# Keys of the later batches split and transposed per chunk in one piece instead of two halves, in a block-sparse attention with a cosine MLP

## The chip, the core and the metric

The kernel runs on one core of a Trainium2 chip. The metric is the device time of one execution in microseconds. TensorE is called PE, VectorE DVE, ScalarE ACT, GpSimd POOL, and SyncE SP; SP issues nearly all DMAs, one after the other, from one queue.

## The reference

```python
batch, n_heads, seq, head_dim = (4, 8, 768, 64)       # block = 32, window = 1, three sampled blocks per row of blocks
scores = scale * np.matmul(q, k.transpose(0, 1, 3, 2))
mask = np.abs(blk_i - blk_j) <= window
mask = mask | (blk_i == 0) | (blk_j == 0) | (blk_i == n_blocks - 1) | (blk_j == n_blocks - 1)
mask[qb * block:(qb + 1) * block, kb * block:(kb + 1) * block] = True      # for the sampled kb of each qb
scores = np.where(mask, scores, -1000000000.0)
attn = np.exp(scores - np.max(scores, axis=-1, keepdims=True))
attn = attn / (np.sum(attn, axis=-1, keepdims=True) + 1e-09)
x = np.matmul(attn, v).transpose(0, 2, 1, 3).reshape(B * S, H * D)         # 3072 x 512
h = x @ w_in                                                               # 512 x 2048
return ((h * np.cos(h)) @ w_out).astype(np.float32)                        # 2048 x 512
```

## The kernel before

**Arithmetic.** Every float32 operand of a matmul is scaled and split into a float16 high part and a float16 remainder, and products are summed from these parts. For keys, `k_hi` writes the high part (ACT, by `hi`, L1274) and `k_lo` the remainder (DVE, by `lo`, L1277) into a tile of the class `kn`, of which there are two; `k_transpose` lets a DMA transpose write the tile into `W`, the transposed keys of the current batch. `W` exists once, so the keys of a new batch replace those of the old one.

**Tiling.** The 768 rows of a batch are six chunks of 128: five sparse ones (chunk 0 to 4 of a batch, numbered 6b to 6b+4 over all batches) and a dense one (6b+5) with the first and last blocks. A sparse chunk has four units of two heads each; a dense chunk has eight units of one head. A unit runs through: scores on PE (`sparse_scores`, L1520 to L1526, or `dense_scores`, L1537), bias and maximum on DVE (L1553), exponential on ACT (L1575), split into high part (ACT, L1585) and remainder (DVE, L1589), a DMA transpose of the probabilities (`PT<-ring`, L1604), and the product with the values (L1614 to L1640). Units 0 and 1 of a sparse chunk use heads 0 to 3 (the first half of `W`), units 2 and 3 use heads 4 to 7. Before a sparse chunk, `k_gather` copies the sampled columns of `W` into `Wg`, partly on DVE and partly on ACT (L1366); for the first chunk of batches 1 to 3 it does so in two halves of four heads.

When two chunks are done, their result is transposed by DMA (`xT<-n`, L1669), and a feed-forward step `m` follows for these 256 rows: per step 16 blocks of 12 matmuls (`up`, L1801), cosine on ACT (L1828) between operations of DVE, and 16 blocks of 6 matmuls (`down`, L1851). There are 12 such steps. Exponential and cosine need different tables on ACT, and each change is an `ACT_TABLE_LOAD`.

**Order.** The program is written out in an order that a planner works out beforehand. `plan_kernel` creates steps with an engine, a cost and a due position; `Plan.run` simulates five engines and always takes, of the steps that could start now, the one with the smallest position. `NUDGES`, a table of some 2700 numbers, shifts the position of each kind of step, of each step number, and of single steps. Each engine executes its own steps in that order and waits wherever a step's inputs or its tile are not ready.

**Exchange of keys.** For batch b+1, `load_k` brings the keys into three `stage` tiles, squares them, spreads the maximum over all partitions with a small matmul (L1305) and makes the scale. `prep_k(b + 1, half, pos)` then creates the split and the transposes: with `half` 0 or 1 for six tiles of 128 keys by four heads, two of which share one `kn` tile; with `half` None (until now only for batch 0) for whole tiles of 128 keys by eight heads. In batch 0 the whole form also has switches for single tiles: other tile classes (`KCL`), the remainder on POOL (`KLP`), and the transpose on PE (`KPE`). The functions that the change touches:

Of the kernel before, what the change touches and what calls it, by code (L numbers as in the profile page):

```python
# [57 lines left out]
    idx=3.61, sx=-0.42, regs=-2.95, regs0=-8.34, regs0_0=-6.69, regs1=6.82, regs1_0=-17.04, regs2=3.29, regs2_0=-20.5, regs0_1=-6.69, const=-17.11,  # L58
    kload=-0.63, kload0=-0.87, kload0_0=-10.62, ksq=9.39, ksq0=-7.31, ksq0_0=-21.27, kload0_1=-7.01, ksq0_1=-41.01, kload0_2=-66.32, ksq0_2=11.5,
    kred=-0.92, kall=1.38, kall0=-31.15, ksc=-0.19, ksc0=-12.07, regs3=21.51, regs3_0=25.08, regs4=9.54, regs4_0=-19.9, regs1_1=-20.28, regs2_1=3.97,  # L60
    regs3_1=-8.55, regs4_1=15.17, vload=9.28, vload0=-15.15, vload0_0=11.52, vsq=-6.11, vsq0=13.32, vsq0_0=4.72, vload0_1=2.59, vsq0_1=-3.92,
    vload0_2=38.86, vsq0_2=14.54, vred=42.82, vred0=3.99, vall=1, vall0=-0.62, vsc=-5.56, vsc0=-4.67, ql=-0.06, ql0=11.94, qsq=-0.33, qsq0=17.87,
    qsc=-3.82, qsc0=1.9, qu=0.12, qnu=-14.73, qnu0=-6.95, qhi=2.68, qlo=2.81, qlo0=1.37, uT=-0.62, uT0=-18.36, up=2.32, up0=11.32, khi=4.75,
    khi0=9.03, klo=14.9, klo0=12.03, kT=-0.1, kT0=-22.55, kT0_2=4.55, kp=4.16, kp0=0.97, kp0_2=2.55, kT0_3=-0.33, kp0_3=6.32, kT0_4=22.41,
    kp0_4=39.57, kT0_5=6.88, kp0_5=4.01, vhi=0.82, vhi0=13.51, vhi0_0=0.77, vlo=6.66, vlo0=-1.79, vlo0_0=32.44, vst=10.44, vst0=38.45, vst0_0=-44.56,
    vhi0_1=-13.35, vlo0_1=34.43, vst0_1=-3.14, vlo0_2=0.6, vst0_2=29, vhi0_3=4.95, vlo0_3=9.17, vst0_3=-0.45, vhi0_4=-0.81, vst0_4=-36.52,
    vhi0_5=3.24, vlo0_5=22.52, vst0_5=5.35, vg=2.22, vg0=-25.12, vg0_0=11.42, vg0_1=3.7, vg0_2=-0.77, vi=-2.42, vi0=-1.84, vi0_0=-2.26, vi0_1=-10.33,
    vi0_2=9.28, vi0_3=23.96, wgd=-0.98, wgd0=-12.88, wga=3.36, wga0=1.25, wl=-2.63, wl0=-13.24, wc=-1.9, wc0=-0.7, wc0_0=8.57, wc0_1=-15.78,
    wc0_2=-17.45, wsq=-0.65, wsq0=-1.13, wl1=6.28, wc1=13.61, wc1_0=9.36, wc1_1=-9.88, wc1_2=-12.47, wsq1=13.17, wl2=-47.49, wl3=-7.45, wc3=3.57,
# [453 lines left out]
def plan_kernel(env, B, H, S, D, DM, DFF, pr):  # L523

    pl = Plan()
# [5 lines left out]
    HH = H // 2  # L531
# [28 lines left out]
    def upos(n, j):  # L560
        return unit_pos[n, j]
# [15 lines left out]
    regs = {}  # L577
# [59 lines left out]
    def prep_k(b, half, pos):  # L637
# [1292 lines left out]
```

## Time and profile before

| what | value |
|---|---|
| runs, not profiled | 857.53, 850.83, 858.05 us (median 857.53) |
| profiled execution, own time | 853.78 us |
| its span, first to last instruction | 851.5 us |
| mean granted clock of PE | 0.936 |
| busy: PE, DVE, ACT, POOL | 727.7, 644.8, 624.8, 101.8 us |
| DMA queue q1 (issued by SP) | 308080 packets, 129.35 MB, 73.1% of 16 engines |
| `ACT_TABLE_LOAD` at L1828, L1575 and L1274 | 18, 17 and 1 of 1283 ns each |
| key splits of four heads, ACT and DVE | 36 each |
| transposes of four heads into `W` | 36 |

In the views below a row names the start and the length in us, the engine, the line and the operation with its output and input tiles; a bracket behind it gives the idle time ahead of it on its engine and what ended that. SPq is SP's queue of issues. Batch 0 is exchanged for batch 1 around 243 to 270 us, for batch 2 around 424 to 454, and for batch 3 around 615 to 645.

### The profile page before, as it was taken

Reading aid. Unit: us, or ns where it says so; the run is one execution under the profiler, and the core shown is the slowest. Engines: PE = TensorE matmul, PEld = TensorE weight load, DVE = VectorE, ACT = ScalarE, POOL = GpSimd, SP = SyncE. Lnnn points to the kernel's source line nnn. Section 1 sums busy time; section 2 is a strip of 40 time slices with the busy share of each in tenths; the row PEclk is TensorE's granted clock in tenths of the full one; section 3 lists DMA queues with packets and bytes.
Section 4 is the critical chain, followed back from the end, with each engine's and each line's share of the span. In section 5 each row is a group of like instructions: output and inputs, shape, how many; then the busy total and the mean of one; then the engine's idle time right before and its main releaser. Section 6 shows DMA issues by size and latency. Waiting matters only on the chain.

```text
span 851.5 us, 23033 instructions
## 1 busy us (share of the span) xinstructions
PE 727.7 (85%) x9272; PEld 506.8 (60%) x9272; DVE 644.8 (76%) x1632; ACT 624.8 (73%) x1193; POOL 101.8 (12%) x128
## 2 busy tenths in 40 slices
PE   3556667779999869987999979999988869999997
PEld 2444554546767537656767548677665548576583
DVE  3999989998967776878668876879578746867352
ACT  1686846888867898788758978779669857769342
POOL 5211231000030101200020111000020111000000
PEclk9965697879999979999999999999999989999999
DMA  9999893398895989899979999989696997855300
GB/s 253 324 208 275 211 264 98 73 233 166 213 222 127 201 164 194 157 230 149 228 159 182 196 177 170 216 133 165 191 156 116 184 196 155 181 83 118 87 2 25
DMA packets 313306, 146.54 MB, mean 172 GB/s; under 512 B 266224, under 2 KB 290928, under 8 KB 313200
## 3 DMA queue, kind: packets, MB, share of 16 engines
q1 hardware_dynamic: 308080, 129.35, 73.1%
q0 software_dynamic: 5120, 15.73, 8.4%
q8 instruction: 72, 1.18, 0.6%
q14 instruction: 34, 0.28, 0.1%
HBM read 68.23 MB, written 12.58 MB: 95 GB/s over the span
## 4 chain that ended last, share of the span: by engine, by line
PE 40%; ACT 12%; DMA 11%; DVE 10%; issue 3%; SPq 1%; DVEq 0%; ACTq 0%
PE ph L1801 19%; PE po L1851 15%; DMA PT<-ring 6%; ACT P L1575 4%; DVE P L1553 3%; DMA W<-kn 2%; DMA xT<-n 2%; ACT ring L1585 2%; DVE ring L1589 1%; PE xp L1640 1%; PE xp L1626 1%; PE sp L1520 1%; DVE hs L1833 1%; DVE g L1842 1%; DVE g L1824 1%
## 5 line engine op out<-in xcount | busy, mean ns | idle before, releaser
L1801 PE MATMUL ph<-xT,w 128*128 128x256 f16 x2304 | 270.8, 278 | 10.1 <-DMA xT<-n 6.7
L1851 PE MATMUL po<-w,g 128*128 128x512 f16 x1152 | 269.0, 383 | 8.6 <-ACT g L1839 7.1
L1801 PEld LDWEIGHTS <-w 128*128 128x128 f16 x2304 | 226.5, 99 | 47.6 <-issue 7.3
L1851 PEld LDWEIGHTS <-g 128*128 128x128 f16 x1152 | 108.2, 98 | 128.0 <-ACT g L1839 7.4
L1575 ACT ACTIVATE P<-P,sm 128x352 f32<-128x352 f32 (+1 forms) x224 | 151.9, 679 | 28.8 <-DVE sm L1570 19.3
L1492 POOL DMA_INDIRECT V<-scr,gidx x80 | 89.2, 1115 | 613.4 <-PE xp L1614 316.0
L1589 DVE TENSOR_TENSOR ring<-P,ring 128x704 f16<-128x704 f32 (+1 forms) x112 | 100.1, 906 | 31.5 <-ACT ring L1585 30.1
L1810 ACT ACTIVATE hs<-ph,sm 128x512 f32<-128x512 f32 x96 | 64.4, 680 | 50.8 <-PE ph L1801 42.8
L1585 ACT CAST ring<-P 128x704 f16<-128x704 f32 (+1 forms) x112 | 86.5, 785 | 13.0 <-DMA PT<-ring 11.9
L1553 DVE CUSTOM_DVE_ANT_1 P<-sp,bias 128x352 f32<-128x352 f32 x160 | 77.7, 518 | 14.1 <-PE sp L1526 13.1
L1833 DVE SCALAR_TENSOR_TENSOR hs<-hs,sm,g 128x1024 f32<-128x1024 f32 x48 | 61.0, 1281 | 23.6 <-ACT g L1828 22.4
L1520 PE MATMUL sp<-W,U 128*128 128x192 f16 x320 | 53.2, 268 | 29.2 <-DVE sm L1553 27.7
L1828 ACT ACTIVATE g<-g,sm 128x1024 f32<-128x1024 f32 x48 | 54.7, 1146 | 23.7 <-DVE g L1824 23.4
L1842 DVE TENSOR_TENSOR g<-hs,g 128x1024 f16<-128x1024 f32 x48 | 58.6, 1223 | 17.1 <-ACT g L1839 16.9
L1839 ACT ACTIVATE g<-hs 128x1024 f16<-128x1024 f32 x48 | 50.4, 1051 | 18.2 <-DVE hs L1833 17.5
L1824 DVE SCALAR_TENSOR_TENSOR g<-g,hs 128x1024 f32<-128x1024 f32 x48 | 58.3, 1220 | 0.5
L1521 PEld LDWEIGHTS <-U 128*128 128x128 f16 x320 | 33.4, 104 | 35.7 <-issue 32.0
L1614 PE MATMUL xp<-V,PT 96*32 96x64 f16 x1920 | 31.0, 202 | 22.0 <-DMA PT<-ring 18.8
L1820 DVE TENSOR_SCALAR g<-hs 128x1024 f32<-128x1024 f32 x48 | 32.9, 691 | 21.8 <-ACT hs L1810 20.1
L1521 PE MATMUL sp<-W,U 128*128 128x64 f16 x320 | 48.7, 207 | 0.0
L1626 PE MATMUL xp<-V,PT 128*128 128x64 f16 x960 | 45.5, 201 | 0.0
L1614 PEld LDWEIGHTS <-PT 96*32 96x32 f16 x1920 | 21.6, 102 | 37.7 <-DMA PT<-ring 25.9
(176 smaller groups left out, 896.0 us busy)
## 6 DMA issues: line engine op xcount, KB each, us to landing
V<-scr SPq DMA_DIRECT2D x20, 384.0 KB
stage<-in_k_dram SPq DMA_DIRECT2D x12, 512.0 KB
w<-in_moe_w_in_dram SPq DMA_DIRECT2D x12, 512.0 KB
w<-in_moe_w_out_dram SPq DMA_DIRECT2D x12, 512.0 KB
V<-scr SPq DMA_DIRECT2D x8, 768.0 KB
scr<-n SPq DMA_DIRECT2D x21, 256.0 KB
qs<-in_q_dram SPq DMA_DIRECT2D x20, 256.0 KB
U<-U SPq DMA_DIRECT2D x40, 128.0 KB
```

Of the source, the lines that this page charges most:

```text
L1492: self.nc.gpsimd.indirect_dma_start(V[:96, 2 + j, :], None, self.scr[b][:, :], bass.IndirectOffsetOnAxis(ap=self.gidx[:96, c : c + 1], axi ...
L1521: mm(spv[:, :, 96:128].rearrange("p y (n c) -> p y n c", c=hf), u, ends, start=False, stop=False)
L1553: self.nc.vector.tensor_tensor_reduce(out=self.p_view(n, Pt)[:, a].rearrange("p (n c) -> p n c", c=hf), in0=sp[:, :w].rearrange("p (n c) - ...
L1575: self.nc.scalar.activation(Pv[:, a], Pv[:, a], AF.Exp, scale=qc[:, 4:5], bias=nb[:, bcol : bcol + 1], accum_out=sums[:, 2 * j + a : 2 * j ...
L1585: self.nc.scalar.copy(R[:, :, 0, : self.width(n)], self.p_view(n, Pt))
L1589: self.nc.vector.tensor_tensor(R[:, :, 1, :w], self.p_view(n, Pt), R[:, :, 0, :w], ALU.subtract)
L1801: self.nc.tensor.matmul(ph[:, ff, :], self.W1[p][:, wl, cc, c * P : (c + 1) * P], xT[:, xl * NCC + cc, :], start=(j == 0), stop=(j == len( ...
L1810: self.nc.scalar.activation(hs[:, h * 512 : h * 512 + 512], ph.rearrange("p f t -> p (f t)"), AF.Copy, scale=self.turns[b][:, p : p + 1])
L1824: self.nc.vector.scalar_tensor_tensor(kt, kt, MAGIC, hs, op0=ALU.subtract, op1=ALU.subtract)
L1833: self.nc.vector.scalar_tensor_tensor(hs, hs, c[:, p : p + 1], kt, op0=ALU.mult, op1=ALU.mult)
L1842: self.nc.vector.tensor_tensor(g[:, 1024:2048], hs, g[:, 0:1024], ALU.subtract)
L1851: self.nc.tensor.matmul(po, g[:, gl, ff, t * P : (t + 1) * P], self.W2[p][:, wl, ff, :], start=(first and ff == half * hf and j == 0), sto ...
```

## The change

`prep_k` of batches 1 to 3 is called once, with `half` None, instead of twice. The switches for single tiles stay confined to batch 0, by `not b` in place of `whole`. So in each later batch 12 splits of four heads become 6 splits of eight heads, on ACT and on DVE, and 12 transposes of four heads become 6 of eight. A tile has its own `kn` tile instead of sharing one. The split of the `Wg` copies into two halves stays.

```diff
-                kn = Val("PT" if whole and pr["KCL"][t] == 0 else "kn")
+                kn = Val("PT" if not b and pr["KCL"][t] == 0 else "kn")
...
-            if whole and pr["KLP"][t]:
+            if not b and pr["KLP"][t]:
...
-            if whole and pr["KPE"][t]:
+            if not b and pr["KPE"][t]:
...
             if i == NS:
-                for half in range(2):
-                    prep_k(b + 1, half, upos(n, HH * (half + 1) - 1) + nudge("F_B", b, 3, 4) + pr["PK"])
+                prep_k(b + 1, None, upos(n, HH - 1) + nudge("F_B", b, 3, 4) + pr["PK"])
```

`NUDGES` is a new table: 2581 of the numbers that stand in both differ, so the order changes everywhere on all engines; `PARAMS` is unchanged. Where its first line begins:

```diff
-    idx=3.61, sx=-0.42, regs=-2.95, ...
+    idx=7.71, sx=20.24, regs=-5.13, ...
```

Line numbers of the operations in the changed kernel are two lower than before.

SP's queue at the third exchange, from the first transpose into `W` on, before (V: values of a chunk from the scratch copy `scr3`; x2: two such instructions in a row):

```order
L1360 DMA_TRANSPOSE W_63<-kn1_88 128x4x128 x2
L1360 DMA_TRANSPOSE W_63<-kn0_87 128x4x128 x2
L1486 DMA V0_105<-scr3_122 16x2048
L1360 DMA_TRANSPOSE W_63<-kn1_88 128x4x128 x2
L1360 DMA_TRANSPOSE W_63<-kn0_87 128x4x128 x2
L1483 DMA V1_106<-scr3_122 96x2048
L1360 DMA_TRANSPOSE W_63<-kn1_88 128x4x128 x2
L1360 DMA_TRANSPOSE W_63<-kn0_87 128x4x128 x2
L1604 DMA_TRANSPOSE PT1_103<-ring0_99 128x12x128
```

And in the changed kernel, from the second transpose into `W` on (the first stands right ahead; qs: queries of a later chunk, out: the output of a feed-forward step):

```order
L1355 DMA_TRANSPOSE W_63<-kn0_87 128x8x128
L1484 DMA V1_106<-scr3_122 16x2048
L1481 DMA V0_105<-scr3_122 96x2048
L1484 DMA V0_105<-scr3_122 16x2048
L1355 DMA_TRANSPOSE W_63<-kn1_88 128x8x128
L1355 DMA_TRANSPOSE W_63<-kn0_87 128x8x128
L1484 DMA V0_105<-scr3_122 16x2048
L1484 DMA V1_106<-scr3_122 16x2048
L1412 DMA qs0_92<-in_q_dram 128x8x64
L1355 DMA_TRANSPOSE W_63<-kn1_88 128x8x128
L1873 DMA out_0_dram<-ot1_111 128x512
L1355 DMA_TRANSPOSE W_63<-kn0_87 128x8x128
```

Twelve issues of four heads became six of eight, loads of V and a load of queries moved in between them, and the store of a finished feed-forward step now stands ahead of the last one.

ACT at the same place before, from the last evacuations of the feed-forward's first matmuls (`hs<-ph`) to the second table load (P: probabilities, ring: their split, g: the cosine):

```order
L1810 ACTIVATE hs_81<-ph_116,sm 128x512
L1810 ACTIVATE hs_82<-ph_115,sm 128x512
L1575 ACT_TABLE_LOAD
L1575 ACTIVATE P_96,sm<-P_96,sm 128x352 x2
L1585 CAST ring_99<-P_96 128x2x352
L1575 ACTIVATE P_98,sm<-P_98,sm 128x352 x2
L1810 ACTIVATE hs_82<-ph_116,sm 128x512
L1585 CAST ring_100<-P_98 128x2x352
L1828 ACT_TABLE_LOAD
L1828 ACTIVATE g_83<-g_83,sm 128x1024
```

And in the changed kernel, from the last step of that feed-forward ahead of the exponentials:

```order
L1837 ACTIVATE g_84<-hs_82 128x1024
L1573 ACT_TABLE_LOAD
L1573 ACTIVATE P_98,sm<-P_98,sm 128x352 x2
L1573 ACTIVATE P_97,sm<-P_97,sm 128x352
L1583 CAST ring_101<-P_98 128x2x352
L1573 ACTIVATE P_97,sm<-P_97,sm 128x352
L1583 CAST ring_99<-P_97 128x2x352
```

Before, two units of the new batch had their exponentials, then the table changed for two cosine steps and back for the third unit. Now all cosine steps of that feed-forward stand ahead of the first exponential, and the next change of the table comes four chunks later.

More of the change, by code (lines that the diff above doesn't have):

```diff
@@ L302 @@
[L302 to L303 removed]
+    idx=7.71, sx=20.24, regs=-5.13, regs0=-7.43, regs0_0=-15.45, regs1=8.54, regs1_0=-15.41, regs2=-3.76, regs2_0=-24.27, regs0_1=-8.84,
+    const=-14.25, kload=-1.1, kload0=-0.53, kload0_0=-3.89, ksq=6.81, ksq0=-3.4, ksq0_0=-11.53, ksq0_1=9.81, kload0_2=-49.06, ksq0_2=-3.48,
+    kred=1.26, kred0=-4.64, kall=1.79, kall0=-48.07, ksc=-1.18, ksc0=-14.2, regs3=0.47, regs3_0=25.15, regs4=19.1, regs4_0=-35.24, regs1_1=-25.92,
@@ new lines @@
+    o1_0=6.1, st1=-6.66, st1_0=14.1, o1_1=0.32, st1_1=-15.83, ql5=0.7, qsq5=4.14, qsc5=2.91, qu5=-11.98, qnu5=1.34, qhi5=0.74, qlo5=13.09,
+    uT5=-12.06, uc5=-26.04, vg5=-0.94, vg5_0=6.71, vg5_1=-32.21, qk4=0.55, mx4=-2.53, nb4=-4.63, nb4_0=-3.92, ex4=-13.95, ex4_0=-10.75, ph4=0.41,
+    ph4_0=3.76, pl4=0.79, pl4_0=10.62, PT4=-8.95, PT4_0=-14.66, pv4=-4.89, pv4_0=-4.5, qk4_1=-1.35, mx4_1=3.71, nb4_1=-2.09, ex4_1=-2.51,
+    ph4_1=-0.23, pl4_1=19.92, PT4_1=-1.11, pv4_1=6.9, qk4_2=1.14, mx4_2=0.43, nb4_2=1.17, ex4_2=-11.87, ph4_2=1.8, pl4_2=-5.24, PT4_2=2.64,
@@ new lines @@
+    gl2_2=-0.36, m2_3=-2.35, ev2_3=-11.93, ka2_3=-6.02, kb2_3=-30.58, sin2_3=0.45, gm2_3=-10.76, gh2_3=44.24, gl2_3=-22.98, d2=-2.53, d2_0=5.85,
+    d2_1=-0.48, d2_2=15.5, d2_3=7.95, o2=11.53, o2_0=6.63, st2=-14.64, o2_1=9.79, st2_1=33.27, ql7=-4.17, qsq7=-6.11, qsc7=-4.89, qu7=2.55,
+    qnu7=-31.7, qhi7=-35.76, uT7=14.11, uc7=30.88, vg7=1.61, vg7_1=11.17, vg7_2=3.29, vi7=-4.79, vi7_0=-5.45, vi7_1=-1.51, vi7_2=-65.41,
+    vi7_3=-11.58, qk6=-6.3, qk6_0=3.88, mx6=-5.11, mx6_0=-10.32, nb6=2, ex6=5.35, ex6_0=0.44, ph6=-5.88, ph6_0=-8.12, pl6=-12.04, pl6_0=-11.7,
@@ new lines @@
+    ex11_1=-30.34, ph11_1=-5.25, pl11_1=1.42, PT11_1=-0.6, pv11_1=36.6, mx11_2=-0.08, ph11_2=-0.45, pl11_2=4.92, PT11_2=-4.29, pv11_2=-55.58,
+    mx11_3=0.39, nb11_3=-0.71, ex11_3=0.33, ph11_3=1.92, pl11_3=-19.07, PT11_3=0.25, pv11_3=-52.55, qk11_4=-0.23, mx11_4=0.35, nb11_4=10.48,
+    ex11_4=-0.4, ph11_4=-1.46, pl11_4=-0.19, pv11_4=1.74, qk11_5=2.21, mx11_5=0.02, nb11_5=-0.15, ex11_5=-36.81, ph11_5=-2.26, pl11_5=-0.89,
+    PT11_5=-0.96, pv11_5=-9.49, qk11_6=2.66, mx11_6=1.42, nb11_6=2.03, ex11_6=-25.07, ph11_6=12.89, pl11_6=-32.44, PT11_6=5.68, pv11_6=8.19,
@@ new lines @@
+    st6_0=-20.25, o6_1=9.5, st6_1=21.31, ql15=-13.19, qsc15=-2.32, qu15=-28.77, qnu15=-20.91, qhi15=-3.25, qlo15=31.99, uT15=1.12, vg15=-9.93,
+    vg15_0=-4.3, vg15_1=7.58, vg15_2=27.23, vi15=-2.36, vi15_0=1.86, vi15_1=-10.46, vi15_2=-8.13, vi15_3=-12.43, qk14=-4.03, qk14_0=-0.47,
+    mx14=-2.52, mx14_0=6.74, nb14=-4.01, nb14_0=2.7, ex14=-0.06, ex14_0=7.59, ph14=9.13, ph14_0=-4.22, pl14=-44.68, pl14_0=-40.57, PT14=-3.87,
+    PT14_0=6.23, pv14=-1.37, pv14_0=1.48, qk14_1=-0.55, mx14_1=4.03, nb14_1=3.64, ex14_1=17.75, ph14_1=-3.54, pl14_1=-27.89, PT14_1=12.11,
@@ new lines @@
+    ql21=-0.09, qsq21=-5.41, qsc21=0.86, qnu21=9.73, qhi21=-14.24, qlo21=10.81, uT21=5.03, uc21=2.33, vg21=-5.58, vg21_0=8.2, vg21_1=-26.3,
+    vg21_2=-18.77, vi21=-0.14, vi21_0=-16.53, vi21_1=-10.88, vi21_2=-23.35, vi21_3=-21.03, qk20=11.75, qk20_0=-2.43, mx20_0=-3.56, nb20=-5.49,
+    nb20_0=3.78, ex20=5.65, ex20_0=4.31, ph20=-9.1, ph20_0=6, pl20=7.41, pl20_0=11.48, PT20=-8.71, PT20_0=4.03, pv20=-6.28, pv20_0=1.18,
+    qk20_1=-6.33, mx20_1=-7.16, nb20_1=1.81, ex20_1=-4.98, ph20_1=-2.83, pl20_1=4.67, PT20_1=0.51, pv20_1=-8.01, qk20_2=-3.94, mx20_2=-9.76,
@@ new lines @@
+    pv23_2=5.79, qk23_3=-0.44, mx23_3=5.51, nb23_3=-4.2, ex23_3=5.9, ph23_3=-0.64, pl23_3=-3.44, PT23_3=-14.74, qk23_4=-0.92, mx23_4=8.81,
+    nb23_4=-1.25, ex23_4=-14.91, ph23_4=-0.75, pl23_4=-25.12, PT23_4=-8.56, pv23_4=1.64, mx23_5=9.02, nb23_5=7.15, ex23_5=-1, ph23_5=3.06,
+    pl23_5=-46.74, PT23_5=15.83, pv23_5=-3.61, qk23_6=3.71, mx23_6=14.99, nb23_6=6.67, ex23_6=13.89, ph23_6=24.81, pl23_6=-6.63, PT23_6=26.4,
+    pv23_6=1.44, qk23_7=24.09, mx23_7=21.41, nb23_7=18.07, ex23_7=7.35, ph23_7=13.64, pl23_7=34.9, PT23_7=27.88, pv23_7=-25.8, rs23=34.43,
@@ L304 @@
+    gh11_3=12.67, gl11_3=8.1, d11=26.16, d11_0=15.36, d11_1=2.45, d11_2=48.44, d11_3=-2.67, o11=18.36, o11_0=-2.22, st11=47.7, st11_0=21.06,
+    o11_1=-0.33, st11_1=46.21,
 )
```

462 lines of the change are left out of this document (216 added, 246 removed).

## Prediction

> **What bounds the kernel now.** I read the page's busy shares first, then its slices, then one table of stretches around the places where the keys of a new batch come in.
>
> ```profile
> PE 727.7 (85%) x9272; PEld 506.8 (60%) x9272; DVE 644.8 (76%) x1632; ACT 624.8 (73%) x1193; POOL 101.8 (12%) x128
> PE   3556667779999869987999979999988869999997
> PEclk9965697879999979999999999999999989999999
> ```
>
> No engine is full over the span: PE stands at 85%. The slices (21.3 us each) show why the mean misleads. Until about 190 us PE is 30 to 70% busy, while weights are loaded and prepared. From there it is at 90% or more, with dips. The dips around 300, 510 and 660 us come once per batch, just behind the exchange of keys:
>
> ```profile
> core 0: us, PE busy (x) PEld busy (x) DVE busy (x) ACT busy (x) POOL busy (x), PEclk, DMA share, GB/s
> 243.00:270.00 27.00, 27.00 (x236) 20.70 (x233) 17.96 (x47) 16.42 (x30) 6.05 (x7) 1.00 0.74 152
> 270.00:325.00 55.00, 43.09 (x809) 26.26 (x806) 43.11 (x142) 49.01 (x111) 8.25 (x8) 0.91 0.96 189
> 424.00:454.00 30.00, 29.61 (x244) 20.42 (x243) 22.79 (x60) 17.23 (x31) 7.13 (x8) 1.00 0.67 154
> 454.00:525.00 71.00, 65.08 (x1034) 44.59 (x1033) 53.98 (x169) 64.34 (x146) 7.36 (x8) 0.95 1.09 193
> 615.00:645.00 30.00, 27.34 (x234) 19.23 (x232) 21.73 (x53) 20.97 (x41) 7.51 (x8) 1.00 0.72 125
> 645.00:700.00 55.00, 41.25 (x758) 25.04 (x756) 40.98 (x147) 43.27 (x101) 7.35 (x8) 0.92 1.00 175
> ```
>
> Rows alternate: the exchange, then what follows. During an exchange PE is full (27.00 of 27.00, 29.61 of 30, 27.34 of 30), because feed-forward blocks of the chunks before are kept for it, and ACT has room (16.42 of 27). Behind it the picture turns: ACT is busy 49.01 of 55 us, 64.34 of 71 and 43.27 of 55, the DMA share is 0.96 to 1.09, and PE idles 11.91, 5.92 and 13.75 us, 31.6 us together. I call these the **starved stretches**: the feed-forward work is used up, and new work comes only when attention has finished two chunks. Such a stretch ends like this:
>
> ```profile
> 694.18 0.36 PE L1614 MATMUL xp<-V,PT 96*32 96x64 f16 x24 [2.53 <-DMA PT<-ring]
> 698.20 7.00 PE L1801 MATMUL ph<-xT,w 128*128 128x256 f16 x47 [3.20 <-DMA xT<-n]
> ```
>
> PE waits for a transposed probability tile, then for xT, and starts the next feed-forward at 698.20. So the change pays only if, behind an exchange, attention gets through its first units sooner. Engine time saved inside an exchange is saved on engines that wait there.
>
> **The engine time removed.** Halves and wholes both have rows:
>
> ```profile
> L1274 ACT ACTIVATE kn<-stage,sm x41: 492/496/734, 14.1 to 636.5; 128x256 f16<-128x256 f32 x36, 128x512 f16<-128x512 f32 x5
> L1277 DVE SCALAR_TENSOR_TENSOR kn<-stage,sm,kn x41: 472/480/752, 15.9 to 638.8; 128x256 f16<-128x256 f32 x36, 128x512 f16<-128x512 f32 x5
> L1360 SPq DMA_TRANSPOSE W<-kn x36: 1188/1216/1789, 246.0 to 640.1; - x36
> L1274 ACT ACTIVATE n<-stage,sm 128x512 f16<-128x512 f32 x18 | 12.5, 716 | 1.3 <-DMA scr<-n 1.3
> L1277 DVE SCALAR_TENSOR_TENSOR n<-stage,sm,n 128x512 f16<-128x512 f32 x18 | 13.1, 747 | 2.1 <-ACT n L1274 2.1
> L1669 SPq DMA_TRANSPOSE xT<-n x23: 1231/1275/2587, 97.0 to 800.4; - x23
> ```
>
> The first three give min/median/max of a half (ns); the last three are the same steps on a tile as large as a whole one. ACT: 36 x 0.496 = 17.9 us become 18 x 0.716 = 12.9, 5.0 less. DVE: 36 x 0.480 = 17.3 become 18 x 0.747 = 13.4, 3.8 less. SP's queue: 36 x 1.216 = 43.8 become 18 x 1.275 = 23.0, 20.8 less. By the table above all three have idle time in the exchanges, so I put this at nothing on the path. Its cover is that idle time; if it were gone, ACT's share would be worth up to 5 us.
>
> **The exchange itself.** The third one, SP first, then what waits on it:
>
> ```profile
> 618.18 5.22 SPq L1360 DMA_TRANSPOSE W<-kn  x4
> 625.56 6.36 SPq L1360 DMA_TRANSPOSE W<-kn  x4
> 635.56 5.74 SPq L1360 DMA_TRANSPOSE W<-kn  x4
> 617.14 1.69 ACT L1274 ACTIVATE kn<-stage,sm 128x256 f16<-128x256 f32 x4
> 624.50 0.51 ACT L1274 ACTIVATE kn<-stage,sm 128x256 f16<-128x256 f32 x1 [1.33 <-DMA W<-kn]
> 632.94 1.00 DVE L1366 COPY Wg<-W 128x128 f16 x8 [1.39 <-DMA W<-kn]
> 647.25 0.88 ACT L1366 COPY Wg<-W 128x128 f16 x4
> ```
>
> There are two kn tiles. The four transposes from 618.18 fill them; the next split waits until 624.50 for the first to land, 6.3 us after its issue. Three such rounds carry the batch. Keys of heads 0 to 3 are complete at 632.94, 15.8 us after the first split (617.14), those of heads 4 to 7 by 647.25, 30.1 us after it.
>
> Whole tiles keep three rounds with two tiles. A round is a split of 0.716 + 0.747 us and a landing L, and the second tile's issue adds 1.3 at the end: 3 x 1.46 + 3L + 1.3 = 5.7 + 3L. Landings of whole tiles:
>
> ```profile
> 557.55 3.31 DMA xT<-n
> 689.98 8.17 DMA xT<-n
> ```
>
> L = 3.31 gives 15.6 us, L = 8.17 gives 30.2. I take L = 6.3, what the half tile took at this very place: 24.6 us. The last keys then come 5.5 us sooner, and the first scores, which now wait for all heads, 8.8 us later.
>
> [...]
>
> **What the new order makes of it.** On PE the order counts feed-forward blocks (12 or 6 matmuls, one block 1.31 or 1.30 us):
>
> ```profile
> 253.22 1.30 PE po L1851 x6
> 254.52 1.31 PE ph L1801 x12
> ```
>
> From the last dense score of the old batch to the third score of the new one (the first on heads 4 to 7) there were 48, 47 and 46 blocks; now there are 49, 49 and 50. To the first score there were 44, 38 and 38; now 47, 46 and 47. So the planner lets the first scores come late, and the third ones 1, 2 and 4 blocks late. PE work as a whole is unchanged; the blocks moved ahead are missing as cover later. What counts is when ACT gets its exponentials:
>
> ```profile
> 441.60 0.25 PE L1520 MATMUL sp<-W,U 128*128 128x192 f16 x1
> 453.54 0.68 ACT L1575 ACTIVATE P<-P,sm 128x352 f32<-128x352 f32 x1
> 648.35 0.25 PE L1520 MATMUL sp<-W,U 128*128 128x192 f16 x1
> 652.73 1.28 ACT L1575 ACT_TABLE_LOAD   x1
> 654.02 0.68 ACT L1575 ACTIVATE P<-P,sm 128x352 f32<-128x352 f32 x1
> ```
>
> *Second exchange.* The first score stood ready at 441.60, and its exponential ran at 453.54: 12 us of head start were not used. Eight blocks later (8 x 1.31 = 10.5) it still comes at 452.1. **0.**
>
> *Third exchange.* The third score came at 648.35, its exponential at 654.02, behind two cosine steps and a table load of 1.28. Now all cosine steps of that feed-forward stand ahead of the first exponential. Four blocks are 5.2 us, of which 2.66 fill the PE idle of 615 to 645; the score comes at 650.9, the maxima add about 1.2, and the exponential runs at 652.1 instead of 654.0. **-1.9.**
>
> *First exchange.* PE was full (27.00 of 27.00), so one block more is one block later. **+1.3**; by the first score, three blocks, it would be +3.9.
>
> The table loads (36 before, 34 after) are in this already, as far as they lie at the third exchange. Of the order elsewhere no row shows a price. It is bounded by the idle time that it could win or add: I allow one starved stretch, 5.9 to 13.75 us, either way, and take 0, since the blocks ahead of each chunk's last score differ by no more than eight anywhere.
>
> Sum: 0 - 1.9 + 1.3 = **-0.6 us** against the profiled execution's 853.78 (span 851.5), so 853.2. The other runs lie 3.75 above it (the median, 857.53), 4.27 above and 2.95 below; I take it as the middle and predict **853 us**.
>
> **Rivals.**
>
> *Slower: late keys starve attention.* The scale of the new keys starts with a small matmul that spreads their maximum:
>
> ```profile
> 614.99 0.22 PE L1305 MATMUL sp<-ident,sm 128*128 128x128 f16 x1
> 404.57 5.60 PE ph L1801 x36
> 522.09 3.94 PE ph L1801 x36
> ```
>
> From it to the first score the new order keeps 20, 25 and 22 blocks, 26, 33 and 29 us. About 3 us of that go to the scale (614.99 to 617.14) and the copies out of W (1.00), so PE has to wait once the exchange lasts longer than 23, 30 and 26 us: L above 5.8, 8.1 and 6.7. (My L of 6.3 makes the first exchange 1.6 us late, as good as the 1.3 above.) At L = 8.17 the three are 7.2, 0.2 and 4.2 us late, 11.6 together. A PE that waits also loses its clock: it falls in the starved stretches (0.91, 0.95, 0.92), and the same 36 matmuls took 5.60 us in one place and 3.94 in another, 1.66 more, once per exchange 5.0. 853.2 + 11.6 + 5.0 = 870; with L = 7.5 (5.2 + 2.2 late) 866. I price it at **867**. For it: 8.17 has been seen, at a DMA share of 1.00, and the last transpose of the third exchange now stands behind an output store on SP. Against: the share in the exchanges is 0.67 to 0.74. [...]
>
> *Faster: the starved stretches shrink.* Behind the third exchange the exponentials of four chunks now run without a cosine step between them, from the first unit on, and the last keys come 5.5 us sooner. If two of the long stretches came down to the 5.92 us of the middle one, 6.0 and 7.8 us would go: **839**. Against: DMA shares near 1.00 there, which the change does not lower.
>
> *Nothing arrives at the end.* The PT and xT transposes set the end of a starved stretch, whatever the keys did: 854 to 857, the noise of the runs.
>
> **How the numbers follow.** My forecast (849 to 859) has 0.40, nothing 0.15, faster 0.24, slower 0.21. A difference of 1% (8.6 us) is about what a measurement of this kernel can tell from none. Faster by over 1% means below 849: 0.24 and 0.05 from the forecast's lower edge, 0.29. Slower means above 866: 0.21 less a part that stays below it, 0.19. The rest, 0.52, is within. The range, 838 to 869, takes in both rivals' middles and leaves out their far ends.
>
> **What would show it.** In the profile after: 18 key splits of about 716 ns on ACT and 747 on DVE; SP issues near 1.28 us; key landings near 6.3; all copies out of W at one time, 24 to 28 us behind the first split; the exponential that follows the third exchange without a cosine step within four chunks; PE idle in each starved stretch within 3 us of 11.9, 5.9 and 13.75. Landings above 7.5, or PE waiting on W in the exchanges, would show the slower rival; idle of 6 us in the first and third stretch the faster one. The forecast is also wrong if the stretch before 200 us, whose order changes little, moves by more than 4 us.

## The result, and the profile after

The changed kernel takes 878.38 us in the median of four runs (876.04 to 881.86), the kernel before 857.06 beside it: a ratio of 1.0268 (95% interval 1.0204 to 1.0332; the ratios are estimated from all runs of a comparison, and differ by up to 0.5% from those of the medians). It is slower, and 878 lies outside the range of 838 to 869. The same kernel with its own order written out as a list (`after_again` and `after_last` below) gave 1.0199 (1.0140 to 1.0257) and 1.0288 (1.0226 to 1.0350). The profiled execution took 876.04 us of its own, with a span of 874.1 (851.5 before) and a mean granted clock of 0.915 (0.936).

A comparison is a set of kernels timed beside each other, and ratios hold within one only: in two of the five later ones, here called **long**, every kernel took about 40 us more (the one before 899.67 and 895.52 us, in the other three, the ordinary ones, 857.48, 856.96 and 855.50), and one chip showed both kinds.

The page after, busy shares, then the clock of PE in slices of 21.9 us:

```profile
PE 738.3 (84%) x9272; PEld 515.0 (59%) x9272; DVE 642.5 (74%) x1614; ACT 619.5 (71%) x1173; POOL 107.4 (12%) x128
PEclk9966688779999976999899999999999688999999
```

DVE and ACT have less work (2.3 and 5.3 us). PE, with the same 9272 matmuls, is busy 10.6 us longer, and the clock shows new low digits (6, where the kernel before has 9) around 340 and 690 us.

The new splits and transposes have the sizes that were forecast. Groups of the changed kernel, the issues and landings of its transposes (batch 0 included), and the first exchange from the first split to the copies out of `W`:

```profile
L1272 ACT ACTIVATE kn<-stage,sm 128x512 f16<-128x512 f32 x23 | 15.8, 714 | 13.1 <-DMA W<-kn 6.8 <-DVE sm L1269 6.3
L1275 DVE SCALAR_TENSOR_TENSOR kn<-stage,sm,kn 128x512 f16<-128x512 f32 x23 | 16.8, 749 | 10.1 <-ACT kn L1272 10.1
L1355 SPq DMA_TRANSPOSE W<-kn x20: 1232/1268/3617, 16.8 to 658.7; - x20
DMA to landing us min/median/max: 3.0/4.9/7.8
251.74 1.33 ACT L1272 ACTIVATE kn<-stage,sm 128x512 f16<-128x512 f32 x2 [2.14 <-DVE sm L1269]
276.43 1.69 ACT L1364 COPY Wg<-W 128x128 f16 x8 [0.68 <-DMA W<-kn]
```

Splits take 714 and 749 ns, an issue 1.268 us, a landing 4.9 in the median and 7.8 at most, and the first exchange 276.43 - 251.74 = 24.7 us. PE never waits for `W` in this trace, so the loss is elsewhere. Here both spans are cut at the same cosines, the first of feed-forward steps 1, 2, 3, 5, 6, 9 and 11 and the second of steps 0 and 8, so that a row of one kernel answers to the same row of the other (from, to, length, PE busy, ..., PEclk, DMA share). Before:

```profile
core 0: us, PE busy (x) PEld busy (x) DVE busy (x) ACT busy (x) POOL busy (x), PEclk, DMA share, GB/s
128.78:219.38 90.60, 73.25 (x837) 48.89 (x838) 86.24 (x228) 74.95 (x151) 1.49 (x1) 0.85 0.67 144
219.38:253.33 33.95, 32.99 (x295) 23.34 (x293) 26.29 (x44) 24.22 (x42) 8.01 (x8) 1.00 0.95 222
253.33:337.99 84.66, 72.75 (x1077) 48.92 (x1076) 62.61 (x192) 72.25 (x157) 8.25 (x8) 0.94 0.89 173
337.99:444.30 106.31, 98.33 (x1198) 69.46 (x1196) 81.09 (x188) 80.81 (x149) 13.14 (x12) 0.98 0.91 189
444.30:524.05 79.75, 73.83 (x1108) 50.15 (x1106) 63.61 (x192) 69.28 (x152) 7.36 (x8) 0.96 1.01 180
524.05:631.65 107.60, 104.95 (x1198) 75.01 (x1196) 81.34 (x171) 79.69 (x138) 12.39 (x12) 1.00 0.89 171
631.65:709.96 78.31, 62.87 (x955) 41.20 (x953) 53.32 (x180) 59.77 (x132) 7.35 (x8) 0.93 0.92 165
709.96:813.91 103.95, 102.55 (x1234) 71.13 (x1232) 69.02 (x134) 72.16 (x115) 4.21 (x4) 1.00 0.57 115
813.91:851.54 37.63, 33.20 (x211) 20.30 (x208) 15.23 (x14) 13.38 (x16) 0.00 (x0) 1.00 0.05 15
```

The changed kernel:

```profile
128.37:225.44 97.07, 73.94 (x842) 48.89 (x843) 86.37 (x228) 75.55 (x150) 1.50 (x1) 0.82 0.70 136
225.44:262.63 37.19, 36.80 (x312) 26.51 (x310) 26.57 (x42) 24.60 (x41) 7.98 (x8) 1.00 0.87 214
262.63:352.06 89.43, 75.94 (x1053) 51.65 (x1052) 62.22 (x188) 68.23 (x149) 7.36 (x8) 0.85 0.80 159
352.06:459.15 107.09, 96.06 (x1152) 67.49 (x1150) 78.70 (x175) 78.14 (x138) 15.01 (x12) 0.97 0.92 193
459.15:540.71 81.56, 74.91 (x1132) 50.59 (x1130) 61.75 (x192) 68.98 (x152) 8.19 (x8) 1.00 0.91 165
540.71:648.43 107.72, 105.00 (x1219) 75.24 (x1217) 81.73 (x173) 82.06 (x141) 13.27 (x12) 1.00 0.85 175
648.43:734.28 85.85, 69.66 (x1028) 47.02 (x1026) 56.48 (x181) 58.61 (x129) 7.74 (x8) 0.84 0.83 141
734.28:835.04 100.76, 99.30 (x1151) 68.84 (x1149) 67.51 (x132) 70.16 (x112) 6.21 (x4) 1.00 0.63 122
835.04:874.11 39.07, 34.99 (x221) 21.34 (x219) 15.53 (x14) 14.68 (x17) 0.00 (x0) 0.98 0.06 21
```

Row by row the lengths differ by +6.5, +3.2, +4.8, +0.8, +1.8, +0.1, +7.5, -3.2 and +1.4; with -0.4 ahead of the first row that is the 22.6 us between the spans. Three places stand out, and they look different. In the first row, before any key of batch 1 is split, PE idles 23.1 us instead of 17.4. In the third and seventh, around the first and third exchange, its idle time hardly grows (11.9 to 13.5, 15.4 to 16.2), but it is busy 3.2 and 6.8 us longer, at a clock of 0.85 for 0.94 and 0.84 for 0.93. The rows do not hold quite the same work: the third has 24 matmuls fewer than before (1053 for 1077), the seventh 73 more (1028 for 955), and the eighth, which is 3.2 us shorter, lacks 83 (1151 for 1234). Part of the +7.5 has thus only moved. The matmuls of the scores alone, of which these two rows have the same 384 in both kernels, show the clock. The rows give from, to and length, PE's busy time on these matmuls, the clock and the DMA share, before and then changed:

```profile
253.33:337.99 84.66, 14.74 (x384) 0.94 0.89 173
631.65:709.96 78.31, 14.86 (x384) 0.93 0.92 165
...
262.63:352.06 89.43, 17.21 (x384) 0.85 0.80 159
648.43:734.28 85.85, 18.15 (x384) 0.84 0.83 141
```

The same scores cost PE 2.5 and 3.3 us more.

The first place, on PE: scores (`sp<-W,U`) of the changed kernel with the waits ahead of them, then the blocks (`ph<-xT,w`) that the kernel before ran between the same scores:

```profile
146.44 0.24 PE L1518 MATMUL sp<-W,U 128*128 128x192 f16 x1 [1.33 <-DVE sm L1551]
149.57 0.32 PE L1518 MATMUL sp<-W,U 128*128 128x192 f16 x1 [2.23 <-DVE sm L1551]
153.04 0.32 PE L1518 MATMUL sp<-W,U 128*128 128x192 f16 x1 [2.02 <-DVE sm L1551]
...
148.20 2.74 PE L1801 MATMUL ph<-xT,w 128*128 128x256 f16 x12
152.17 4.10 PE L1801 MATMUL ph<-xT,w 128*128 128x256 f16 x36
```

The new order puts four scores in a row. Each waits until DVE has emptied the one PSUM tile for scores, and the feed-forward blocks that could fill the wait stand behind them. At the other two places the reverse is seen: blocks run out. PE's down blocks of the changed kernel shortly ahead of the block-free stretch behind the third exchange and right behind it, the 144 up matmuls right behind the one of the first exchange, and the two block-free stretches as windows; last, the same 144 up matmuls in the kernel before:

```profile
665.28 2.76 PE L1849 MATMUL po<-w,g 128*128 128x512 f16 x12
696.81 3.61 PE L1849 MATMUL po<-w,g 128*128 128x512 f16 x12
340.52 17.37 PE L1799 MATMUL ph<-xT,w 128*128 128x256 f16 x144
...
313.06:340.52 27.46, 15.88 (x385) 12.58 (x384) 16.27 (x59) 15.25 (x36) 3.68 (x4) 0.56 1.04 193
670.18:696.81 26.63, 16.55 (x433) 13.19 (x431) 18.69 (x68) 21.10 (x53) 3.67 (x4) 0.71 0.91 165
...
327.93 15.90 PE L1801 MATMUL ph<-xT,w 128*128 128x256 f16 x144
```

For 27.5 and 26.6 us PE has attention alone, and the granted clock falls to 0.56 and 0.71; the longest such stretch of the kernel before behind 200 us is 11.8 us (297.10 to 308.91). Right behind the stretches twelve down matmuls take 3.61 us instead of the 2.76 shortly ahead, and 144 up matmuls 17.37 for 15.90. PE's idle time in the first stretch is eight waits of 11.6 us together, the longest 3.69, in the second seven of 10.0, the longest 2.96. Whether the clock answers to them is not shown.

### The profile page after: what moved, and what is told of

Read it like the earlier page. It is cut to its first block, busy times and chain, and to the rows that moved or that the text cites. A ratio compares the mean times of both kernels' runs of the same rounds, so it can differ in the third digit from the quotient of the medians.

```text
span 874.1 us, 22959 instructions
## 1 busy us (share of the span) xinstructions
PE 738.3 (84%) x9272; PEld 515.0 (59%) x9272; DVE 642.5 (74%) x1614; ACT 619.5 (71%) x1173; POOL 107.4 (12%) x128
## 4 chain that ended last, share of the span: by engine, by line
PE 45%; DMA 23%; DVE 18%; ACT 7%; issue 4%; DVEq 1%; SPq 1%; POOL 0%; ACTq 0%
PE ph L1799 19%; PE po L1849 16%; DMA PT<-ring 15%; DVE P L1551 2%; DMA xT<-n 2%; PE xp L1624 2%; ACT P L1573 2%; DMA stage<-in_k_dram 2%; PE sp L1518 2%; PE sp L1535 2%; DVE w L1275 2%; PE xp L1638 1%; DVE ring L1587 1%; PE xp L1612 1%; DMA w<-in_moe_w_in_dram 1%
## 5 line engine op out<-in xcount | busy, mean ns | idle before, releaser
L1799 PE MATMUL ph<-xT,w 128*128 128x256 f16 x2304 | 274.2, 279 | 7.8 <-DMA xT<-n 3.2
L1490 POOL DMA_INDIRECT V<-scr,gidx x80 | 95.1, 1189 | 633.9 <-PE xp L1612 325.9
L1583 ACT CAST ring<-P 128x704 f16<-128x704 f32 (+1 forms) x112 | 86.0, 786 | 14.6 <-DMA PT<-ring 14.1
L1518 PE MATMUL sp<-W,U 128*128 128x192 f16 x320 | 55.6, 275 | 27.0 <-DVE sm L1551 25.6
L1840 DVE TENSOR_TENSOR g<-hs,g 128x1024 f16<-128x1024 f32 x48 | 58.6, 1223 | 11.8 <-ACT g L1837 11.5
L1837 ACT ACTIVATE g<-hs 128x1024 f16<-128x1024 f32 x48 | 50.4, 1051 | 15.4 <-DVE hs L1831 14.8
L1818 DVE TENSOR_SCALAR g<-hs 128x1024 f32<-128x1024 f32 x48 | 33.0, 691 | 24.6 <-ACT hs L1808 24.6
L1519 PE MATMUL sp<-W,U 128*128 128x64 f16 x320 | 50.9, 212 | 0.0
L1624 PE MATMUL xp<-V,PT 128*128 128x64 f16 x960 | 47.8, 205 | 0.1
```

Source lines behind the costliest of these rows:

```text
L1490: self.nc.gpsimd.indirect_dma_start(V[:96, 2 + j, :], None, self.scr[b][:, :], bass.IndirectOffsetOnAxis(ap=self.gidx[:96, c : c + 1], axi ...
L1518: mm(spv[:, :, 0:96], u, keys[:, :, 64 * i : 64 * i + 96], start=(z == 0), stop=False)
L1519: mm(spv[:, :, 96:128].rearrange("p y (n c) -> p y n c", c=hf), u, ends, start=False, stop=False)
L1583: self.nc.scalar.copy(R[:, :, 0, : self.width(n)], self.p_view(n, Pt))
L1624: mm(xp[:, h, :], PT[:, 6 * a + 3 * l + c, :], V[:, c, h, d0:d1], start=False, stop=(a == 1 and c == 1 and x == len(terms) - 1),)
L1799: self.nc.tensor.matmul(ph[:, ff, :], self.W1[p][:, wl, cc, c * P : (c + 1) * P], xT[:, xl * NCC + cc, :], start=(j == 0), stop=(j == len( ...
```

## The experiments

**Keys or order?** Both kernels with an order that is written out instead of planned. A list `ORDER` gives every step its place, and the planner's choice is replaced:

```diff
+        for o, x in zip(ops, ORDER):
+            o.pos = x
...
-                    if t > lim + delta:
+                    if o.pos != len(order):
                         continue
```

In `whole_in_old` the list is the order of the kernel before; in `half_in_new` that of the changed kernel.

> Whole keys (six splits and six transposes per batch), everything else in the old order: each whole step stands where the first of its two halves stood, and only what needs the later keys (two copies out of W, the first scores with their maxima and exponentials) moves behind other steps. Theory 'order': the 20 us come from the new order, the whole keys by themselves are worth nothing: within 1% of before, 850 to 863. Rival 'keys': whole keys make the first scores of each batch late and starve attention, 5 to 8 us per exchange: 870 to 882, as the changed kernel.

> Keys in halves, everything else in exactly the order of the changed kernel: where a whole step stood, its two half steps stand. Theory 'order': as slow as the changed kernel, 870 to 882. Rival 'keys': the halves bring the time back to before, 853 to 862.

Measured, in a long comparison: 1.0022 (0.9982 to 1.0061) and 1.0084 (1.0051 to 1.0117). Both were repeated where the kernel before takes 857 us:

> Whole keys in the old order again, now beside the changed kernel. Theory 'order': 0.995 to 1.006 of before on any chip, and at least 1% faster than the changed kernel beside it. Rival 'keys': within 0.5% of the changed kernel.

> Keys in halves in exactly the order of the changed kernel, now on whatever chip this is. On a chip with 857 us for the kernel before, the changed kernel is 1.020 to 1.027. The new order keeps 47, 46 and 47 blocks ahead of the first score, so that whole keys are in time there. Theory 'order': halves change little, 1.015 to 1.03. Rival 'keys': halves give back what whole keys cost in the old order, 1.010: 1.010 to 1.015. On a chip with 900 us it was 1.008.

Measured: 1.0098 (1.0057 to 1.0139), 866.85 us, and 1.0264 (1.0198 to 1.0330), 884.17 us. The second is the clear one: **with the keys in halves, the new order alone loses as much as the changed kernel** does in its three comparisons (1.0199 to 1.0288). Its first, third and seventh row are like those of the changed kernel (97.07, 89.43 and 85.85), the third 3.5 us longer:

```profile
129.68:226.60 96.92, 73.15 (x842) 48.20 (x843) 86.45 (x228) 75.49 (x150) 1.49 (x1) 0.82 0.70 137
...
263.94:356.83 92.89, 76.40 (x1052) 51.38 (x1051) 62.87 (x191) 68.93 (x150) 7.36 (x8) 0.89 0.80 153
...
654.00:740.09 86.09, 68.75 (x1018) 46.66 (x1017) 56.91 (x183) 59.11 (x132) 7.76 (x8) 0.84 0.82 143
```

It has the block-free stretches too, 26.1 and 27.2 us long (from 318.67 and 676.10); in `whole_in_old_2` the longest behind 200 us is 11.8.

The first is against my expectation: whole keys in an order made for halves cost 1%, less than the rival 'keys' had said, but not nothing.

**Where in the order?** Spliced lists, whole keys: one order up to the first key split of batch 1 (the last run: of batch 3), the other behind.

> Whole keys. The old order up to the first key split of batch 1 (about 245 us), the order of the changed kernel from there on. Where the loss is by stretches: in the trace the changed kernel is 6 us late at 225 us already (cosine of the second feed-forward step) and 9 at 253, so if a loss that has been made is kept, 9 us come back: 866 to 872. If a late start is made good behind (PE has idle time in the starved stretches), nothing comes back: 874 to 882.

> Whole keys. The order of the changed kernel up to the first key split of batch 1, the old order from there on. If a loss that has been made is kept: whole keys in the old order plus 6 to 9 us, 860 to 870. If the late start is made good behind: as whole keys in the old order, 850 to 863.

Measured, long comparison: 1.0001 (0.9963 to 1.0039) and 1.0182 (1.0128 to 1.0236). There the new start costs 1.6% and the new order behind it nothing. The other kind of comparison says the opposite:

> The changed kernel itself, once more, as the measure for the runs beside it. The first comparison of old and new order ran on a chip on which the kernel before takes 900 us, not 857. There whole keys in the old order were 1.002 of before, the new order up to the exchange alone added 0.016, the new order behind the exchange alone added nothing. If these add up, the changed kernel is 1.014 to 1.018 of before on such a chip; if the two pieces of the new order harm each other, or the chip makes no difference, it is 1.02 to 1.033 as in the first measurement.

> Whole keys, old order up to the first key split of batch 1, new order behind, again beside the changed kernel. If the loss lies in the start alone: 0.995 to 1.005 of before. If the new order behind the exchange also costs on this chip (in the first trace of the changed kernel 16 of the 22.6 us arise behind 245 us): 1.012 to 1.02.

> Whole keys, the old order up to the first key split of batch 3 (about 617 us), the order of the changed kernel from there on. Old order throughout is 1.010, new order from batch 1 on is 1.0265. In the traces 4.3 of the 10.7 us between them arise in the third exchange and its starved stretch, where the new order has 11 feed-forward blocks between the first score and the next feed-forward step, and the old one 16. Theory 'cover spent early': about 1.014 to 1.017. If the stretches before set the difference: 1.008 to 1.012. If the third stretch alone sets it: 1.02 to 1.027.

Measured: 1.0199 for the changed kernel, 1.0265 (1.0184 to 1.0346) for the old start with the new order behind it, 1.0168 (1.0119 to 1.0217) for the old order up to batch 3. So the old start takes its 6 us back at 220 us, and they are gone at the end. Between the second and the third run lie 9.0 us (878.55 and 869.54), the new order from the first key split of batch 1 to that of batch 3; but these runs belong to two comparisons, and their intervals overlap. From the third to whole keys in the old order (866.85) it is 2.7 more, within the intervals. The pieces do not add up, and they weigh differently in the long comparisons; that is as far as splicing goes.

**One engine's order put back.** In `new_pe_old` the list is that of the changed kernel, but PE's steps between 144 and 205 us stand as before (four scores no longer in a row).

> The changed kernel with one stretch of one engine's order put back: from the third to the ninth unit of chunks 3 to 5 (about 144 to 205 us), PE takes scores, products with V and feed-forward blocks in the old order, where a block stands behind nearly every score; in the new order four scores stand in a row and wait for their PSUM tiles, with blocks behind them that could run. Theory 'PE queue': PE stands idle at the head of its queue, so this gives back most of the 6 us that are lost by 225 us: 0.6% faster than the changed kernel, the second feed-forward's first cosine 4 to 6 us earlier. Rival 'other queues': the loss comes from SP's order (transposes of P and xT) or from ACT and DVE, whose order is as in the changed kernel: no difference over 0.2%.

Measured: 1.0454 (1.0389 to 1.0519), 20 us **slower** than the changed kernel beside it. Its second feed-forward has its first cosine at 247.57 us instead of 227.25. DVE and ACT still take their steps in the new order and now wait longer at the head of their queues: between 130 and 250 us DVE 13.0 us for scores (6.5 in `after_again`), ACT 22.5 us for the maxima that DVE makes from them (8.7). PE in turn waits up to 10.1 us for weights that DVE has yet to split. Neither theory said so: here one queue's part of an order could not be judged alone.

**Why do whole keys cost 1% in the old order?** In `whole_in_old_2` PE waits for `W` in the first exchange (its first score, then its first exponential, then that of the kernel before):

```profile
271.13 0.20 PE L1646 MATMUL sp<-W,U 128*128 128x64 f16 x1 [1.51 <-DMA W<-kn]
274.38 0.68 ACT L1700 ACTIVATE P<-P,sm 128x352 f32<-128x352 f32 x1 [1.02 <-DVE sm L1695]
...
270.11 0.68 ACT L1575 ACTIVATE P<-P,sm 128x352 f32<-128x352 f32 x1 [0.53 <-DVE sm L1570]
```

The first exponential is 4.3 us late. This is the mechanism of my slower rival, in an order that keeps fewer blocks ahead of the first score. More tiles for the keys should remove it (here the version with six; those with three and five name PT for tiles 2 and 5, and for 1, 3 and 5):

```diff
-                kn = Val("PT" if not b and pr["KCL"][t] == 0 else "kn")
+                kn = Val(("kn", "PT", "kn", "PT", "n16", "PT")[t] if b else "PT" if pr["KCL"][t] == 0 else "kn")
```

> Whole keys in the old order, but tiles 2 and 5 of each later batch are split into a tile of the class PT (probabilities), which lies idle during an exchange, so that three splits and transposes go out per round and the keys are done in two rounds instead of three. No other step changes its place. Whole keys in the old order cost 1.010 of before: in their trace PE waits for W ahead of the first score of batch 1 (1.87 and 1.51 us) and the first exponential comes 4.3 us late. Theory 'late keys': two rounds of 2.9 + 6.3 with two more issues of 1.3 are about 20 us, less than the 22 that the old order leaves, so the wait goes and with it all of the loss: 0.994 to 1.003 of before, no wait of PE for W over 0.3 us. Rival 'bigger pieces': the loss comes from the whole transposes themselves (the queue and the landings behind them), not from when the keys are complete: 1.007 to 1.012 as with two tiles.

> As the run with three tiles, but tiles 1, 3 and 5 of the keys lie in PT, so that five splits and transposes can go out at once and only the fifth waits for the first to land. Theory 'late keys': once the keys are in time, more tiles bring nothing, because the order of PE's blocks ahead of the first score is fixed: within 0.3% of the run with three tiles. If the keys still come late with three: 0.5% faster than that.

Measured: 1.0105 (1.0064 to 1.0146) and 1.0097 (1.0060 to 1.0135). With five tiles the first exponential of batch 1 comes at 270.83 us, 0.7 late instead of 4.3, but the loss comes back by the next exchange, where the last transpose stands behind a store and a load of V on SP and PE waits for it:

```profile
444.14 1.24 SPq L1482 DMA_TRANSPOSE W<-PT  x1
...
447.87 0.20 PE L1646 MATMUL sp<-W,U 128*128 128x64 f16 x1 [2.51 <-DMA W<-PT]
```

> Whole keys in the old order, each of the six tiles in a tile of its own (kn, PT, kn, PT, n16, PT), all six splits and transposes where the first two stood, ahead of the loads of V and of the output store that follow on SP. With five tiles the first exchange lost nothing (first exponential of batch 1 0.7 us late instead of 4.3), but in the second one the last transpose stood behind an output store and a load of V on SP (issued at 444.14, 12.5 us after the first), and PE waited 2.51 us for W; the third exchange lost 5 us in the same way. Theory 'late keys': with all six up front, no exchange waits for W, and the 1% goes: 0.995 to 1.004 of before. Rival 'something else in whole keys': 1.007 to 1.012 again.

> Whole keys in the old order with six tiles, beside the changed kernel. On a chip with 895 us for the kernel before it was 0.9945 of before, with no wait of PE for W. Theory 'late keys': on a chip with 857 us, where two tiles cost 1.010 and five 1.0097, it is 0.992 to 1.003, and 2% faster than the changed kernel. Rival 'something else in whole keys': 1.007 to 1.012 there, and the gain on the other chip is of that chip.

Measured: 0.9945 (0.9912 to 0.9978) in a long comparison, and 1.0076 (1.0034 to 1.0117), 863.28 us, where before is 855.50 and the changed kernel 879.48. The waits of PE for `W`, 2.3 us in `whole_in_old_2`, are down to this:

```profile
PEld L1646 <- DMA W<-PT: 1.1, 1, 1.1
PE sp L1646 <- DMA W<-PT: 0.7, 1, 0.7
```

The waits are nearly gone, and the ratio is 1.0076 instead of 1.0098, within the intervals: in the ordinary comparison the rival 'something else in whole keys' held. Late keys made the first exponential late, but that they cost the 1% is not shown. The largest piece of the loss is now in another place, between the first cosines of steps 3 and 5, where the kernel before takes 106.31 us:

```profile
339.75:452.08 112.33, 101.27 (x1200) 70.18 (x1198) 82.03 (x186) 80.45 (x144) 14.60 (x12) 0.97 0.94 189
```

PE is busy 2.9 us longer there and idle 3.1 us longer; why stays open. Six tiles beat the changed kernel by 2%, and the kernel before only in the long comparison.

**Blocks, clock or waits?** `spread_1` moves four of six down blocks of the changed kernel into the block-free stretch behind the first exchange. `warm_new` and `warm_old` add matmuls of no use:

```diff
+        for _ in range(warm):
+            mm(xp[:, h0, :], self.ident, self.ident[:, 0:D], start=True, stop=True)
```

> The changed kernel with six feed-forward blocks of one place moved on PE: behind the first score of chunk 8 the new order runs six down blocks in a row and then has nine scores and ten products with V without a block between them; now two stand there, and four stand between the later scores. Nothing else moves on any other engine. Theory 'attention alone cools PE': the granted clock between the first cosines of steps 2 and 3 (0.85, where the old order has 0.94) rises above 0.88, and the stretch, 89.4 and 89.7 us in two traces, gets 1 to 4 us shorter. Rival 'waits': blocks between scores only delay the scores; clock and stretch stay as they are.

> The changed kernel with work added: ahead of each product with V of chunks 7, 8, 18, 19 and 20 (20 units), PE runs 12 matmuls of 128x64 with the identity into the unit's own place in PSUM, which the product then overwrites; by the same shape in the product, 12 of them are 0.52 us. They run while PE waits for the transposed probabilities. Theory 'cold clock': in the stretches of the first and third exchange the granted clock rises from 0.85 and 0.84 to over 0.90, the stretches (89.4 and 85.9 us) get 2 to 5 us shorter each, the whole 1.010 to 1.02 of before instead of 1.020 to 1.027. Rival 'waits set it, the clock follows': the added work costs what it takes, 0.5 us a unit where PE did not wait: up to 10 us more, 1.025 to 1.038.

> The kernel before with the same 12 added matmuls in the same units. There the clock in these stretches is 0.94 and 0.93. Theory 'cold clock': little to win, 0.992 to 1.002 of before; if the added work only costs: 1.004 to 1.012.

Measured, long comparison: 1.0051 (1.0011 to 1.0090), 1.0017 (0.9977 to 1.0058) and 1.0045 (1.0006 to 1.0084). The first and third exchange in `spread_1`, then in `warm_new`:

```profile
272.96:364.64 91.68, 76.90 (x1067) 51.08 (x1066) 62.03 (x188) 68.46 (x150) 7.63 (x8) 0.89 0.77 155
668.20:750.34 82.14, 67.97 (x1025) 46.36 (x1023) 56.48 (x181) 58.46 (x130) 7.53 (x8) 0.85 0.80 146
...
266.57:357.43 90.86, 78.69 (x1141) 53.89 (x1139) 62.07 (x188) 68.48 (x149) 7.36 (x8) 0.92 0.83 157
660.99:747.30 86.31, 72.03 (x1153) 50.24 (x1151) 56.70 (x181) 58.49 (x130) 7.77 (x8) 0.88 0.80 138
```

The added work raises the clock from 0.85 and 0.84 to 0.92 and 0.88. The spread blocks shorten the block-free stretch behind the first exchange from 27.5 to 13.4 us and raise the clock of that row to 0.89, as expected. But the row of the first exchange is in neither run shorter than the 89.43 us of the changed kernel; these are traces of a long comparison, so the lengths are no fair measure. In the kernel before, the added 20 x 0.52 = 10.4 us of work cost 0.45%, about 4 us. The changed kernel was to be measured beside them:

> The changed kernel once more, as the measure beside the run with six tiles, and for spread_1 and warm_new, which ran on a chip on which the kernel before takes 895 us (1.005 and 1.002 of before). If this is such a chip and the added matmuls and the moved blocks did nothing, the changed kernel is 1.000 to 1.006 there, and the whole loss depends on the chip; if they helped, it is 1.01 or more. On a chip with 857 us for the kernel before it is 1.02 to 1.027 again.

It fell on an ordinary comparison: 1.0288. So the changed kernel has no time in the long kind, and these two runs have no measure. That the lower clock goes with the loss is seen; that it is its cause is not shown.

## Why the prediction was wrong

- **The keys themselves: sizes right, the length of the exchange in part by luck.** Splits 716 and 747 ns forecast, 714 and 749 measured; issues 1.275 and 1.268. The first exchange took 24.7 us for 24.6 forecast, but the parts differ: L was 4.9 in the median, not 6.3, which would give 20.4, and the third round did not wait for a landing. ACT starts its two splits at 269.78 without a wait, straight behind feed-forward steps. The other two exchanges took 27.5 and 25.1. PE never had to wait for `W` in a way that the trace shows, so the slower rival did not happen in the changed kernel; its waits appeared in `whole_in_old_2`.
- **The three exchanges by blocks up to the first or third score: wrong.** Forecast +1.3, 0 and -1.9, together -0.6; the rows that begin in an exchange (the third, fifth and seventh) give +4.8, +1.8 and +7.5, together 14.1 (in the other two traces of the changed kernel +5.1 and +5.2, +4.4 and +0.5, +3.8 and +8.9). The count ended at the first scores. What was lost lay behind them: the new order leaves PE 27 us of attention without a block at two exchanges. I had written that blocks moved ahead are missing as cover later, and gave it no price.
- **"Of the order elsewhere no row shows a price ... and take 0": this step failed.** The other rows, with the 0.4 us ahead of them, add 8.5 us, and `half_in_new_2`, the new order without whole keys, takes 1.0264 of before, where my whole sum for keys and order was -0.6 us. What in the order costs this is seen only in part (scores in a row, stretches without a block, a lower clock) and not shown as the cause. That the blocks ahead of each chunk's last score differ by at most eight says nothing of which steps stand next to each other. One starved stretch, 5.9 to 13.75 us, was no bound either, since the new table moved every stretch.
- **"PE work as a whole is unchanged":** in matmuls yes, in time no. It is busy 10.6 us longer.
- **The stretch before 200 us**, which was to stay within 4 us, lost 6.5 by 225 us. I had named this as a sign of a wrong forecast, and it was one, although with the old start (`old_then_new_2`) the end came no sooner.
- **ACT:** the exponentials of the third exchange run without a cosine step between them, as forecast, but the first comes at 667.71 us, 27.7 later than before (640.05), where the row that holds it starts 16.8 late. The one of the third unit, forecast 1.9 us sooner, comes at 674.22 instead of 654.02: 20.2 late, 3.4 more than the start of its row.

## What to carry to other kernels

When an edit comes with a newly worked out order, the order is the larger unknown: price every stretch that it moves, not the place of the edit, and widen the range by the sum. Count not only how many filler blocks stand ahead of a point, but the longest stretch without one and the scores that wait in a row. An edit is best tried with the old order first, replayed step by step: here it cost 1% there, and the new order hid that.

## What the hardware showed beyond that

The same kernel on the same chip took 890.83 us in one comparison and 863.28 in another (`keys_6_tiles`). The traces differ in waits of an engine that no event in the profile ends (issue) or that end by a queue which it does not know (remote). The three rows are the longest two of the long one and the longest of the other, with total, times and longest in us:

```profile
PEld L1646 <- issue: 43.7, 28, 6.6
DVE P L1678 <- remote: 24.8, 7, 5.2
...
PEld L1646 <- issue: 32.3, 25, 3.0
```

Summed over all engines but POOL they are 174.3 and 73.3 us; in all traces of ordinary comparisons 66 to 77, in those of the long ones 130 to 187. What holds the engines up there is not in the profile. It also changes verdicts: half keys in the new order are 1.0264 of before in one kind and 1.0084 in the other.
